# A written order for the prelude and two batches of a Nyström attention and mixture kernel, without filler products

## The chip, the core and the metric

The kernel runs on one core of a Trainium2 chip. The metric is the device time of one execution in microseconds (us). Lower is better. Times of several runs are given as their median.

## What is computed

Three blocks follow one another; their sizes are those of the inputs.

```python
# attention: q, k, v are (8 batches, 8 heads, 576 positions, 64)
q_lm, k_lm = mean of q, k over groups of 18 positions          # 32 landmarks
A, Bm, C = softmax(q k_lm'/8), softmax(q_lm k_lm'/8), softmax(q_lm k'/8)
Z = Bm' / (norm1(Bm) * norminf(Bm) + 1e-6)
for _ in range(6): Z = 2*Z - Z @ Bm @ Z                        # Newton steps
x = A @ Z @ C @ v                                              # as (4608, 512)
# gated block: d_ff = 1536
x = (silu(x @ w_gate) * (x @ w_val)) @ w_out
# soft mixture: 8 experts, 4 slots each
logits = x @ phi;  d = softmax over the tokens, c = softmax over the slots
slot_input = d.T @ x;  slot_out = relu(slot_input[e] @ w1[e]) @ w2[e]
out = c @ slot_out
```

## The kernel before

The work goes through eight batches. A prelude computes the attention of batch 0 (`first_attention`, L424): landmark sums on DVE (`landmark`, L393), score products on TensorE (`scores`, L602; tiles `m_a`, `m_c`), exponentials on ACT, the norm product `m_nx` (L521), five Newton squares (`m_n`, L533) with their side products (`m_T`, L554 and L555), the products with v (`m_v`, L481), and at the end `w_blocks` (L596), which leaves the small matrix `WB`. Beside it runs `a_softmax` (L770): maximum, subtraction on POOL (L792), exponential, sums, multiplication on POOL (L795), a transpose on DVE into `AT` (L789), a copy `EH` rounded by ACT (L797) and the rest `EL` by POOL (L798).

A batch then has twelve units (`unit`, L1020). A unit multiplies the weight product `G` (`g_product`, L812; `GH` by ACT in L837, `GL` by DVE in L851) with `EH` and `EL`: six products into `pg` and six into `pv` for each half (`mm3`, L1011), a gate on ACT (L375) and a product on DVE into `hT` (L1046, or L1044). `logits` (L857) multiplies `hT` for tile `l`. A transpose of `hT` (L871) puts the batch's block into the buffer `HB`. Inside the units of batch b run pieces of the attention of batch b+1 (`attention`, L609) and of the slot sums of batch b-1 (`softmoe`, L902). In batch 0 the weights are converted from double precision as well (`f32_bits`, L237: lines L248, L251 and L252 on DVE, L235 and L242 on ACT), and `w_out` is folded with phi (`m_wt`, `m_p`, `m_ps`; L328, L337, L343).

The slot sums (L985) are 72 products of 32 rows by 32 columns of the array. A product has a place a (which 32 rows) and g (which 32 columns), 16 places in all, and a step k. It takes its part of the exponentials: the tile `DN` itself where a equals g, otherwise a copy in `DR` (the end of buffer `HB_85`) that one of twelve small transfers on the SP queue brought (L951). The transfers are numbered by i = a xor g from 1 to 3 and by a.

SP issues nearly all loads in the order of its instructions; one that has to wait holds those behind it. The other engines are in order too. For the first part of the program a table, `ORDER` (L55), lists for each engine the order of its instructions by their number in the traced program; `written_order` (L123) makes a chain of them. In the kernel before it covers 906 TensorE instructions, 257 on DVE, 180 on ACT, 18 on POOL and 71 on SP, that is the prelude and batch 0. From there to the end the instructions of batch 1 and of the later batches follow the order that the scheduler finds with a few fences.

Filler products: `keep_warm` (L875) multiplies 128 by 128 with 160 columns into a tile nobody reads. `first_attention` calls it four times with four products (L505). At the start 16 products of one element are issued (L1091).

Of the kernel before, what the change touches and what calls it, by code (L numbers as in the profile page):

```python
# [53 lines left out]

ORDER = {  # L55
    'PE': '''
# [7 lines left out]
      788+4 820+6 832+8 814+6 826+6 844+12 862+6 872+16 856+6 888+8 840+4 896+6 920+8''',  # L64
    'DVE': '''
# [8 lines left out]
      239 242+2 238 241 240 247+2 255 252 256+2 253 259 249 246 258 262 261''',  # L74
    'Activation': '''
# [5 lines left out]
      162 167 166 168+2 171 173 170 174 172 175 181 177 176 180 179''',  # L81
    'Pool': '''
      0 2+6 1 8 10 9 11 16 12 15 13+2 17''',
    'SP': '''
      0+2 5 2+2 7 4 6 14 26 8 15 18 10 25 22 17 16 20 9 23 11+3 40 24 19 21 29+2 28 32+2 31 34 36 35 37+3
      42 41 58 43 45 44 27 46 59+2 47+2 61 50+2 49 64 52 65 53 56+2 66+2 54 68+3 55 62 71''',
}


# [1 line left out]
def nystrom_softmoe_kernel(  # L91
# [332 lines left out]
    def first_attention(side):  # L424
# [18 lines left out]
        def c_scores(half):  # L443
            ms = [psp.tile([128, 512], F32, tag="x", name="m_c", bufs=3) for r in range(2)]
            scores(ms, qs, "k", b, half, range(4))
            return ms
# [55 lines left out]
        for r in range(2):  # L502
            c_copy(r, 0, cm[r])
        cm = c_scores(1)
        for _ in range(4):  # L505
            keep_warm(4)
        side("a")
        for r in range(2):
# [366 lines left out]
    def keep_warm(n):  # L875

        m = psp.tile([128, 512], F32, tag="l", name="warm")
        for _ in range(n):
            pe.matmul(m[:, 0:160], ident, cst[:, 128:288], start=True, stop=True)  # L879
# [208 lines left out]
                next(gens[c], None)  # L1088

    m = psp.tile([128, 512], F32, tag="l", name="warm")  # L1090
    for _ in range(16):  # L1091
        pe.matmul(m[0:1, 0:1], one, one, start=True, stop=True)
    first_attention(side)
    in_order("silu", warm, one, AF.Silu)
    for f in side_pre:
# [328 lines left out]
```

## Time and profile before

| | us |
|---|---|
| median of 3 runs (lowest, highest) | 652.75 (651.09, 653.97) |
| profiled execution, its own time | 652.49 |
| its span from first to last instruction | 650.5 |
| prelude, until the first `pg` product | 38.64 |
| batch 0 | 76.27 |
| batch 1 | 69.04 |
| batches 2 and 3 | 65.16, 65.15 |
| busy share of TensorE, DVE, ACT, POOL | 95%, 72%, 46%, 11% |

The stages are cut at the first `pg` product of each batch. The profile gives the busy time of each engine, the clock granted to TensorE, waits by who ended them, and the instructions in order of time. A busy share is an average over stages with different limits, so each stage is read by itself.

### The profile page before, as it was taken

The page shows a single profiled execution, that of the slowest core. Times are in us where ns is not written, and L with a number is a line of the kernel's source. Part 1 is how long each engine was busy: PE and PEld are TensorE (multiplying, and loading weights), DVE is VectorE, ACT ScalarE, POOL GpSimd, SP SyncE. Part 2 cuts the span into 40 slices and gives each one's busy share as a digit, 9 for nine tenths or more (in the row PEclk, how much of TensorE's full clock was granted, in tenths as well). Part 3 has the DMA queues.
Part 4 walks back from the last instruction along what each step waited for, and adds up shares of the span by engine and source line. Part 5 has one row for each costly group of instructions (what it writes and reads, how often), then busy time and mean ns, then how long its engine had stood idle before and what let it go on. Part 6 is the DMA issues. An engine that isn't in the chain of part 4 may idle for free. (4 is left out here: it accounts for less than half of the span.)

```text
span 650.5 us, 18267 instructions
## 1 busy us (share of the span) xinstructions
PE 616.0 (95%) x7591; PEld 465.9 (72%) x7591; DVE 465.8 (72%) x1139; ACT 300.8 (46%) x761; POOL 73.2 (11%) x81
## 2 busy tenths in 40 slices
PE   6889999999999999999999999999999999999990
PEld 3766787777878787878787878787878877743660
DVE  5999898797679687868786878687866555540441
ACT  2787885374256225622562256225723532410540
POOL 0310003021013001300130013001300000010100
PEclk9999999999999999999999999999999999999996
DMA  9997861443042024202420242022310696599999
GB/s 335 390 350 260 341 219 56 164 137 96 7 143 90 2 76 145 90 2 76 145 90 3 74 145 87 6 74 75 100 49 2 218 365 236 191 329 347 348 369 318
DMA packets 63298, 106.47 MB, mean 164 GB/s; under 512 B 4976, under 2 KB 33008, under 8 KB 61680
## 3 DMA queue, kind: packets, MB, share of 16 engines
q1 hardware_dynamic: 63216, 105.32, 48.0%
q8 instruction: 59, 0.97, 0.6%
q14 instruction: 23, 0.19, 0.1%
HBM read 91.24 MB, written 12.58 MB: 160 GB/s over the span
## 5 line engine op out<-in xcount | busy, mean ns | idle before, releaser
L375 ACT ACTIVATE u<-pg 128x288 f32<-128x288 f32 x169 | 69.8, 413 | 152.2 <-PE pg L1017 147.4
L1046 DVE TENSOR_TENSOR hT<-u,pv 128x288 f32<-128x288 f32 x169 | 75.7, 448 | 41.1 <-PE pv L1017 34.9
L1017 PE MATMUL pg<-EH,GH 128*128 128x288 f32 x384 | 92.9, 323 | 0.0
L851 DVE TENSOR_TENSOR GL<-g,GH 128x512 fp32r<-128x512 f32 (+1 forms) x114 | 65.0, 597 | 35.3 <-ACT GH L837 35.3
L1017 PE MATMUL pg<-EH,GL 128*128 128x288 f32 x384 | 84.5, 297 | 0.5
L1017 PE MATMUL pv<-EH,GH 128*128 128x288 f32 x384 | 84.0, 300 | 0.0
L1017 PE MATMUL pg<-EL,GH 128*128 128x288 f32 x384 | 82.1, 295 | 0.0
L1017 PE MATMUL pv<-EL,GH 128*128 128x288 f32 x384 | 82.0, 295 | 0.0
L1017 PE MATMUL pv<-EH,GL 128*128 128x288 f32 x384 | 81.9, 294 | 0.0
L837 ACT CAST GH<-g 128x512 fp32r<-128x512 f32 (+1 forms) x114 | 53.8, 520 | 55.6 <-PE g L820 55.6
L1017 PEld LDWEIGHTS pg<-EH,GH 128*128 128x128 f32 x384 | 59.4, 189 | 23.6 <-issue 20.4
L871 DVE STREAM_TRANSPOSE HB<-hT 128x576 f32<-128x576 f32 x96 | 74.2, 774 | 1.6
L1017 PEld LDWEIGHTS pg<-EH,GL 128*128 128x128 f32 x384 | 62.0, 188 | 2.6 <-DVE GL L851 2.6
L1017 PEld LDWEIGHTS pv<-EH,GH 128*128 128x128 f32 x384 | 61.2, 188 | 3.7 <-issue 2.5
L1017 PEld LDWEIGHTS pv<-EH,GL 128*128 128x128 f32 x384 | 61.5, 188 | 0.0
L1017 PEld LDWEIGHTS pg<-EL,GH 128*128 128x128 f32 x384 | 61.5, 188 | 0.0
L1017 PEld LDWEIGHTS pv<-EL,GH 128*128 128x128 f32 x384 | 61.5, 188 | 0.0
L820 PE MATMUL g<-w,WB 64*32 64x512 f32 (+1 forms) x912 | 55.5, 534 | 1.9 <-DVE GL L851 1.0
L866 PE MATMUL l<-hT,P_sb 128*32 128x160 f32 (+1 forms) x768 | 44.6, 297 | 2.6 <-DVE hT L1046 1.6
L866 PEld LDWEIGHTS l<-hT,P_sb 128*32 128x32 f32 x768 | 15.4, 108 | 40.7 <-DVE hT L1046 14.6
L985 PE MATMUL m_d<-HB,HB 32*32 32x384 f32 x864 | 35.3, 491 | 0.0
L985 PE MATMUL m_d<-HB,DN 32*32 32x384 f32 x288 | 35.1, 491 | 0.0
(254 smaller groups left out, 943.4 us busy)
## 6 DMA issues: line engine op xcount, KB each, us to landing
k<-in_kT_dram SPq DMA_DIRECT2D x52, 288.0 KB, 3.8
ffn<-in_w_dram SPq DMA_DIRECT2D x13, 1024.0 KB, 8.8
ffn<-in_w_dram SPq DMA_DIRECT2D x24, 512.0 KB, 9.0
HB<-in_w_cat_dram SPq DMA_DIRECT2D x8, 1024.0 KB, 8.2
v<-in_v_dram SPq DMA_DIRECT2D x8, 1024.0 KB, 5.9
q<-in_qT_dram SPq DMA_DIRECT2D x28, 288.0 KB, 2.9
HB<-in_w_out_dram SPq DMA_DIRECT2D x12, 512.0 KB, 5.1
wr<-in_w_cat_dram SPq DMA_DIRECT2D x4, 1024.0 KB, 7.6
```

The source lines that it names most:

```text
L375: i = act.activation(*a, **kw)
L820: pe.matmul(gs[r][32 * hp:32 * hp + 32, 0:256 * n].rearrange("p (u f) -> p u f", u=n), WB[b % 2][64 * r:64 * r + 64, hp, :], w[64 * r:64 * ...
L837: act.copy(H_, g)
L851: dve.tensor_tensor(out=GL, in0=g, in1=GH, op=ALU.subtract)
L866: pe.matmul(L[32 * c:32 * c + 32, 0:32 * k], P_sb[:, j, :], main[:, 0:k, c, :], start=j == 0, stop=j == NJ - 1)
L871: dve.transpose(HB[b % 2][:, S * j:S * j + S].rearrange("p (t r) -> p t r", r=32), hT[:, 0:S].rearrange("p (t r) -> p t r", r=32))
L985: pe.matmul(ms[a][32 * g:32 * g + 32, 0:384].rearrange("p (j f) -> p j f", j=NJ), d_of(a, g, k), hb[32 * a:32 * a + 32, :, 4 * k + g, :], ...
L1017: pe.matmul(ps[:, 0:HALF], G_t[b, j, q, sel_][h], e[:, q, ts_], start=n == 0, stop=n == 5)
L1046: i = dve.tensor_tensor(out=o, in0=u, in1=pv[:, 0:HALF], op=ALU.mult)
```

## The change

The table `ORDER` is replaced. It now covers 1306 TensorE instructions, 352 on DVE, 236 on ACT, 22 on POOL and 94 on SP: the prelude, batch 0 and nearly all of batch 1. The 72 slot sums of batch 0, which run inside batch 1, are among them, each by its own number. The 16 filler products of the prelude are gone; the row of one-element products at the start has 31 instead of 16. No instruction that computes something is added or removed, and everything behind the table stands as before.

```diff
 ORDER = {
     'PE': '''
-      0+48 56+4 48+8 60+15 77+4 75+2 81+3 93 84+4 94 88+4 119 95+4 120 92 121+4 99+20 145+2 125+20 147+4
...
+      967+2 993+8 975+12 955+4 987+6 1005+40 1052+6 1064+6 1045+7 1001+4 1058+6 1070+7 1079 1077+2 1081
+      1080 1083 1087 1084 1091 1095 1085 1099 1082 1088 1103 1092 1086 1090 1107 1096 1094 1111 1089 1115
...
         cm = c_scores(1)
-        for _ in range(4):
+        for _ in range(0):
             keep_warm(4)
...
     m = psp.tile([128, 512], F32, tag="l", name="warm")
-    for _ in range(16):
+    for _ in range(31):
         pe.matmul(m[0:1, 0:1], one, one, start=True, stop=True)
```

All lines of the changed kernel stand 14 lines lower. Three places of the order follow.

TensorE in the prelude, from the second half of the `m_c` scores to the first Newton square; before:

```order
L606 MATMUL m_c<-qk_102,qs 32x288 x2
L879 MATMUL warm<-cst 128x160 x12
L521 MATMUL m_nx<-nrm,cst 128x128
L533 MATMUL m_n<-bd 128x128 x2
L471 MATMUL m_t<-cst,CE_161 128x128 x4
L533 MATMUL m_n<-newton 128x128 x2
```

and now:

```order
L620 MATMUL m_c<-qk_102,qs 32x288 x2
L547 MATMUL m_n<-bd 128x128
L535 MATMUL m_nx<-nrm,cst 128x128
L547 MATMUL m_n<-bd 128x128
L485 MATMUL m_t<-cst,CE_176 128x128 x4
L547 MATMUL m_n<-newton 128x128 x5
```

The fillers between the scores and `m_nx` are gone, and so are four that stood between the two halves of the scores.

SP's queue in batch 1, around the twelve transfers from `DN` for the slot sums of batch 0 (`k3`, `q3`, `v3` are loads for batch 3); before:

```order
L219 DMA q3_0_2432<-in_qT_dram 128x576
L219 DMA q3_1_2434<-in_qT_dram 128x576
L219 DMA q3_2_2436<-in_qT_dram 128x576
L951 DMA HB1_85<-DN_81 32x160 x12
L224 DMA v3_2169<-in_v_dram 128x4x512
L225 DMA v3_2169<-in_v_dram 64x512
```

and now, after three of the twelve and the loads of `k3_2` and `k3_3`:

```order
L965 DMA HB1_85<-DN_81 32x160 x4
L233 DMA q3_0_2427<-in_qT_dram 128x576
L239 DMA v3_2164<-in_v_dram 64x512
L320 DMA wo_dram_88<-HB1_85 128x512
L965 DMA HB1_85<-DN_81 32x160 x3
L233 DMA q3_1_2429<-in_qT_dram 128x576
L965 DMA HB1_85<-DN_81 32x160 x2
```

Five of the twelve transfers now stand behind the load of `v3`, whose buffer comes free when the product of batch 2's attention with v (`m_v`, L724) is done.

TensorE in batch 1, the first slot sums (the four tiles `m_d` stand for a = 0 to 3, and `DN` as second operand means a = g); before:

```order
L985 MATMUL m_d_2230<-HB0_84,DN_81 32x384
L985 MATMUL m_d_2231<-HB0_84,HB1_85 32x384
L985 MATMUL m_d_2232<-HB0_84,HB1_85 32x384
L985 MATMUL m_d_2233<-HB0_84,HB1_85 32x384
L985 MATMUL m_d_2230<-HB0_84,HB1_85 32x384
```

and now:

```order
L999 MATMUL m_d_2225<-HB0_84,DN_81 32x384
L999 MATMUL m_d_2228<-HB0_84,HB1_85 32x384
L999 MATMUL m_d_2226<-HB0_84,HB1_85 32x384
L999 MATMUL m_d_2227<-HB0_84,HB1_85 32x384
L999 MATMUL m_d_2226<-HB0_84,DN_81 32x384
L999 MATMUL m_d_2225<-HB0_84,HB1_85 32x384
L999 MATMUL m_d_2228<-HB0_84,HB1_85 32x384 x2
```

Before, the products went through all 16 places in turn. Now the sequence is irregular; the seventh and eighth share a = 3, with g = 1 and g = 2, and the eighth reads the transfer i = 1, a = 3, which is the last of the twelve in SP's new order.

## Rows read from the trace of the kernel before

**Rows 1.** The page: span, busy time of TensorE, granted clock in 40 slices.

```profile
span 650.5 us, 18267 instructions
...
PE 616.0 (95%) x7591; PEld 465.9 (72%) x7591; DVE 465.8 (72%) x1139; ACT 300.8 (46%) x761; POOL 73.2 (11%) x81
...
PEclk9999999999999999999999999999999999999996
```

**Rows 2.** Stages: stretch, length, busy PE, PEld, DVE, ACT, POOL; clock, DMA share, GB/s.

```profile
0.00:38.64 38.64, 28.67 (x344) 20.36 (x344) 30.30 (x72) 20.65 (x46) 9.68 (x13) 1.00 0.98 369
38.64:114.91 76.27, 74.29 (x851) 58.08 (x845) 70.19 (x162) 56.76 (x131) 8.99 (x8) 1.00 0.66 234
114.91:183.95 69.04, 67.22 (x866) 51.80 (x866) 54.36 (x134) 31.19 (x83) 10.61 (x10) 1.00 0.33 105
183.95:249.11 65.16, 64.99 (x826) 51.09 (x825) 51.19 (x127) 29.35 (x77) 8.29 (x8) 1.00 0.25 78
```

**Rows 3.** TensorE's waits in batch 0: total us, times, longest us.

```profile
PE m_ps L343 <- ACT HB L338: 1.3, 1, 1.3
PE g L820 <- DVE GL L851: 1.0, 1, 1.0
```

**Rows 4.** TensorE's waits in batch 1.

```profile
PE l L866 <- DVE hT L1046: 1.0, 1, 1.0
PE l L866 <- DVE hT L1044: 0.6, 1, 0.6
```

**Rows 5.** Busy time in the part of batch 0 with the conversions.

```profile
40.00:100.00 60.00, 58.02 (x695) 44.88 (x692) 56.82 (x134) 48.83 (x111) 3.82 (x3) 1.00 0.76 272
```

**Rows 6.** Timeline of TensorE, prelude: start, length, line, out<-in, count, idle before.

```profile
5.14 1.17 PE L606 MATMUL m_a<-q,ks 64*32 64x288 f32 x4 [3.33 <-DVE ks L396]
...
15.29 4.18 PE L879 MATMUL warm<-cst 128*128 128x160 f32 x24
19.53 0.49 PE L521 MATMUL m_nx<-nrm,cst 128*128 128x128 f32 x2
...
39.01 0.43 PE L1017 MATMUL pg<-EL,GH 128*128 128x288 f32 x2
```

**Rows 7.** Timeline of DVE, ACT and POOL, prelude.

```profile
16.08 0.39 DVE L517 TENSOR_SCALAR nrm<-cst,stat 128x32 f32<-128x32 f32 x2
...
17.90 0.74 DVE L457 TENSOR_REDUCE stat<-CE 128x1 f32<-128x576 f32 x1
...
21.02 0.61 DVE L544 SCALAR_TENSOR_TENSOR newton<-m_n,rc,cst 128x128 f32<-128x128 f32 x2
...
28.76 1.44 DVE L789 STREAM_TRANSPOSE AT<-AN 128x576 f32<-128x576 f32 x2 [0.79 <-POOL AN L795]
...
33.82 0.46 DVE L591 TENSOR_SCALAR VD<-m_v,rc 128x64 f32<-128x64 f32 x2
...
35.42 1.69 POOL L798 TENSOR_TENSOR EL<-AT,EH 128x576 fp32r<-128x576 f32 x1
```

**Rows 8.** Clock: tile m_c (min/median/max ns), stretches of the Newton steps and the end.

```profile
L606 PE MATMUL m_c<-k,qs x16: 402/555/686, 10.8 to 14.9; 64*32 64x288 f32 x16
...
20.50:34.00 13.50, 11.95 (x154) 10.08 (x154) 12.41 (x33) 10.63 (x25) 4.01 (x4) 1.00 1.03 410
...
638.00:640.00 2.00, 0.00 (x0) 0.00 (x0) 0.00 (x0) 0.00 (x0) 0.00 (x0) 0.50 1.09 386
```

**Rows 9.** The transfers from DN in batch 1: issue ns, landing, then SP's timeline.

```profile
L951 SPq DMA_DIRECT2D HB<-DN x12: 582/588/1817, 138.1 to 146.3; - x12
...
DMA to landing us min/median/max: 1.8/2.1/3.7
...
146.98 0.53 SPq L224 DMA_DIRECT2D v<-in_v_dram  x1
```

**Rows 10.** TensorE in batch 1: product with v, then the stretch of the slot sums.

```profile
144.57 1.73 PE L724 MATMUL m_v<-v,CT 128*32 128x64 f32 x80
...
151.90:156.20 4.30, 4.30 (x144) 2.49 (x144) 1.00 0.37 98
```

More of the change, by code (lines that the diff above doesn't have):

```diff
@@ L56 @@
     'PE': '''
[7 rows of a table removed]
-      788+4 820+6 832+8 814+6 826+6 844+12 862+6 872+16 856+6 888+8 840+4 896+6 920+8''',
-    'DVE': '''
[8 rows of a table removed]
-      239 242+2 238 241 240 247+2 255 252 256+2 253 259 249 246 258 262 261''',
-    'Activation': '''
[5 rows of a table removed]
-      162 167 166 168+2 171 173 170 174 172 175 181 177 176 180 179''',
[14 rows of a table added]
+      1288+16''',
+    'DVE': '''
[12 rows of a table added]
+      342 341 350 352+2 318''',
+    'Activation': '''
[7 rows of a table added]
+      231 227+3 232 230 211 233 235 234 236''',
     'Pool': '''
-      0 2+6 1 8 10 9 11 16 12 15 13+2 17''',
+      1 0 2+5 8 7 10 9 11 13 12 15+2 14 18 17 20 19 23''',
     'SP': '''
-      0+2 5 2+2 7 4 6 14 26 8 15 18 10 25 22 17 16 20 9 23 11+3 40 24 19 21 29+2 28 32+2 31 34 36 35 37+3
-      42 41 58 43 45 44 27 46 59+2 47+2 61 50+2 49 64 52 65 53 56+2 66+2 54 68+3 55 62 71''',
+      0+4 5+3 4 25 18 8 17 23 15 9 16 26 22 19 10 14 11+2 21 32 40 20 29 13 30 24 33 31 36 34+2 37 58 28
+      39 42 41 38 59 43+2 27 45 48 47 46 60 51 50 53 52 61 49 55 64 56 65 54 57 62 66+8 81 87 82 74+2 77
+      84 76 83 90 89 63 85+2 78 91 80 79 88 92+2''',
 }
```

50 rows, old and new, of the table ORDER are left out of this document.

## Prediction

> **What bounds the kernel now.** I read the page first: TensorE is busy 616.0 of 650.5 us and its granted clock is full in all slices but the last [rows 1]. An average says nothing about a stage, so I cut the run at the first `pg` product of each batch [rows 2]. The reader is to see four numbers there: the prelude takes 38.64 us with TensorE busy for 28.67, batch 0 takes 76.27, batch 1 69.04, and batch 2 65.16, as do the batches that follow it. From batch 2 on TensorE has 0.2 us of idle time in a batch; there it is the bound, and nothing of it is changed. So what the change gains or loses must be decided before 183.95 us, and arrives at the end unchanged: the order behind it is the same, and the next piece of work is released by the progress of TensorE.
>
> How much is to be had before that point? Batch 1 is 3.88 us longer than batch 2, and the waits of TensorE that the trace names in it are two of `l` for `hT`, 1.0 and 0.6 us [rows 4]. Batch 0 has conversions to do as well: between 40 and 100 us DVE is busy 56.82 of 60 us [rows 5], so DVE and TensorE are both nearly full, and only the 3.18 us in which DVE stands idle can be taken out by order alone. TensorE's two large waits there, 1.3 for `m_ps` and 1.0 for `g`, are of that size [rows 3]. In the prelude TensorE is idle for 10 us, but the chain of small steps is what lasts: norms, Newton steps, `VD`, `WB`, `G`, and beside it the softmax that ends in `EL`.
>
> **The change part by part.** The profiled execution took 652.49 us by its own time; the median of the three runs is 652.75, so the sum below stands 0.26 under what it would be from the median. That is less than the runs differ by.
>
> *Fillers.* The last input of the norm product is written on DVE by 16.47 (two instructions from 16.08, 0.39 together), but TensorE works through 24 filler records from 15.29 to 19.47 and only then starts `m_nx` at 19.53 [rows 6, 7]. DVE had other work to do in those 3 us, reductions of `AN` and `CE`, so the loss is smaller: in the new order three reductions of 576 elements (0.74 each), the two `newton` instructions (0.61) and small ones of some 1.3 in all stand between the last norm input and the end of the second `newton` tile, 4.1 us, and that tile was written at 21.63 before. The Newton steps would begin at about 20.6, 1.0 us earlier. They don't carry this over to the first unit in full. On DVE the two transposes into `AT` (1.44 us), which ran at 28.76, now stand behind `VD`. `VD` ended at 34.28; 1.0 earlier is 33.3. A conversion of some 0.6, the first transpose (0.7), its copy by ACT (0.6) and two `EL` of up to 1.69 on POOL follow, which makes 38.6 for the second `EL`, or 38.3 if the first takes only 1.4. The product that reads it stood at 39.01 [rows 6, 7]. I take **-0.6 us** for the prelude; the bounds are -1.0 (nothing waits for `EL`) and 0.
>
> *One-element products.* 15 more. TensorE stands idle for 3.33 us before the first scores, behind these products, until DVE has a landmark sum [rows 6]. **0**, hidden by the loads and that sum; without this cover they would cost less than 1.
>
> *Clock.* Without the fillers TensorE has almost no work between the end of the scores near 15 and the first Newton square near 20. The same product `m_c` took 686 ns at the beginning and 402 later [rows 8]; I read the long one as the lower level (1.2 GHz), although the profile's clock says 1.00 there. At the end of the run, with TensorE idle after 636, the granted clock is 0.50, which is 1.2 GHz [rows 8]. So an idle stretch can cost the clock, and the Newton steps would start at half rate. From 20.5 to 34 TensorE is busy for 11.95 of 13.50 us [rows 8], but in the new order ACT and DVE set the first steps, with conversions and exponentials between the copies, so a few us at half rate cost little. I take **+0.5**, between 0 and the case below. The Trainium skill, on its page TensorE: Matmul & The Clock Gate (Part 1), says that the low clock is the default, that activity lifts it and that idleness brings it back; it advises against idle gaps between bursts, and so speaks against this change. By the page alone the whole Newton part could begin at the low clock, which is the second rival's time instead of +0.5.
>
> *Batch 0, new order on five engines.* The same instructions, so the same busy time. Bounds: -3.2 (DVE never idle) and 0, or a loss if a wait is planned wrongly (the last rival covers losses). I take half, **-1.6**, because the order of before was written out too and still left 2.3 us of waits on TensorE.
>
> *Batch 1, now written.* Bounds: -3.9 (it becomes like batch 2) and 0. I take the two named waits, **-1.6**.
>
> *Slot sums of batch 0.* Two prices. First the transfers: the eighth product needs the last of the twelve transfers. Five of them stand behind the load of `v3` on SP, which waits for the end of `m_v`. In the trace `m_v` ended at 146.30 [rows 10]. From there SP issues the load of `v3` and two more (0.53 each, by the row of the load of v), and three, then one, of the small transfers (588 ns each) before it issues the last: 1.6 + 2.35 = 3.9 us, and 2.1 until it lands, 6.0 in all [rows 9]. TensorE reaches the first slot sum sooner. Before, it had 24 products of a unit, one `l` and one Newton step between 146.30 and 151.90, 5.6 us with a wait of 1.0 [rows 4, 10]; now the same 24 products and one `l` more (0.3), which is 4.9. Everything behind the eighth product waits, as the engine is in order: 6.0 - 4.9 = **+1.1**, bounds 0.8 and 2.7 by the fastest and slowest landing (1.8 and 3.7). Second the places: 72 products in turn over 16 places took 4.30 us, that is 4.5 rounds of 0.96 [rows 10]. The new sequence breaks into eight runs in which no place repeats (10, 12, 12, 9, 8, 6, 12 and 3 products). If each run cost a round, the last a third of one, it would be 7.0 us, +2.7; if a repeated place cost nothing, 0. I take **+0.7**, nearer the lower end, because a repeated place is held up only by the one product that is still in it.
>
> Sum: -0.6 + 0.5 - 1.6 - 1.6 + 1.1 + 0.7 = -1.5, and 652.49 - 1.5 = **651.0 us**.
>
> **The rivals.**
>
> *The plan holds everywhere.* Prelude -1.0, batch 0 -3.2, batch 1 -3.9, slot sums and clock at 0: 652.49 - 8.1 = 644.4 us. For it: batches 2 to 6 show that this instruction mix runs at 65.2 with TensorE never waiting. Against it: DVE at 95% in batch 0, and the queue of SP as counted above. Chance 0.30, with times from 644 to 649.
>
> *The clock stays low in the Newton steps.* Place: TensorE from 20.5 us on. Price: 11.95 us of products at half rate are 23.9, 10.4 more than the 13.5 that the stretch has, so 652.49 - 2.0 + 10.4 = 660.9 us, the -2.0 being the other terms. If the clock returns in the middle, 655.7. It decides from the point where half-rate products fill the stretch, that is if the clock is low for longer than 3 us beyond 20.5. Against it: scores and fillers in the trace ran at the long duration at first and were at the short one after some 5 us of work, and Newton products are nearly as dense. Chance 0.11; slower.
>
> *Slot sums block TensorE.* The last transfer lands late (+2.7) and each run costs a round (+2.7), and batch 1 gains nothing elsewhere: 652.49 - 1.7 + 5.4 = 656.2 us. For it: the counts above. Against it: in the trace the first products of the next round start before all of the last have ended. Chance 0.10, a third of it within the bound of no change.
>
> **How the numbers follow.** About 0.5%, 3.3 us either side of 652.75 (649.5 to 656.0), is what a measurement can tell from no change. My forecast, 651.0, has 0.49; its own range is 648.5 to 654, and 0.06 of its chance lies under 649.5. Faster: 0.30 + 0.06 = 0.36. Same: 0.43 + 0.03 = 0.46. Slower: 0.11 + 0.07 = 0.18. The range reaches from the floor of the first rival (644) past the third (656.2) and over the half-way case of the clock, to 657; outside lie most of the full clock case and the unlikely gains beyond every bound, less than 2 in 10.
>
> **What would show it.** Right: `m_nx` near 17 and the second `newton` tile near 20.6; the first `pg` near 38; batch 0 near 74.7, batch 1 near 69.2, batch 2 still 65.2; a gap on TensorE after the seventh slot sum that a transfer ends, and a stretch of slot sums over 5 us. Wrong on the clock: `m_n` and `m_T` records of the Newton steps twice as long for more than 3 us, or a row of clock 0.50 between 15 and 38. Wrong on the slot sums: all of them within 4.3 us of the first. Wrong altogether: batch 2 no longer at 65.2, since then something behind the table has moved.

## The result and the profile after

The changed kernel takes 661.2 us (median of 4 runs, 659.07 to 663.47), the kernel before in the same comparison 653.18 us (651.09 to 653.97). The ratio is 1.0134, its 95% interval 1.0117 to 1.0151: slower by 1.3%, where 651.0 with a range to 657 was predicted and slower had a chance of 0.18. The profiled execution took 661.36 us, 8.9 more than that of before.

The page of the changed kernel: span, busy time, granted clock.

```profile
span 659.5 us, 18273 instructions
...
PE 620.0 (94%) x7589; PEld 467.9 (71%) x7589; DVE 466.4 (71%) x1139; ACT 300.8 (46%) x761; POOL 73.0 (11%) x81
...
PEclk9788999998999999999999999999999999999996
```

The clock line, all nines before [rows 1], now has a 7 and three 8s besides the last slice: something before 66 us and near 160 us lowers the clock. The stages, cut at the first `pg` product of each batch, answer to [rows 2]:

```profile
0.00:39.49 39.49, 28.92 (x351) 19.25 (x351) 30.96 (x75) 21.07 (x47) 9.59 (x13) 0.89 0.97 351
39.49:119.92 80.43, 75.37 (x848) 59.23 (x845) 69.64 (x160) 56.38 (x130) 8.88 (x8) 0.97 0.67 236
119.92:193.61 73.69, 69.93 (x860) 53.77 (x858) 54.66 (x133) 30.89 (x83) 10.54 (x10) 0.98 0.29 89
193.61:258.74 65.13, 64.96 (x827) 51.06 (x825) 51.31 (x127) 29.38 (x77) 8.30 (x8) 1.00 0.25 78
```

The prelude is 0.85 us longer, batch 0 4.16, batch 1 4.65; batch 2 is as it was. These make 9.7 us; the stretch from the start of batch 2 to the end gives 0.7 back (465.9 against 466.6 us). Its instructions are the same in all runs, yet it lay between 465.5 and 469.0 us in their profiled executions. In three stages the clock column stands below 1.00. The stretches in question, in the same view:

```profile
16.70:23.50 6.80, 6.09 (x22) 4.88 (x23) 6.61 (x18) 5.94 (x10) 2.94 (x3) 0.50 1.01 407
37.20:40.60 3.40, 3.40 (x28) 1.70 (x27) 2.73 (x6) 3.01 (x7) 1.92 (x2) 0.51 1.01 385
57.60:61.10 3.50, 3.50 (x28) 2.35 (x27) 2.89 (x7) 2.72 (x5) 1.47 (x1) 0.52 0.93 226
160.00:163.50 3.50, 3.50 (x75) 2.35 (x65) 0.18 (x1) 0.00 (x0) 0.04 (x1) 0.52 0.87 331
```

Four times the clock falls to its lower level, 1.2 GHz, while TensorE has work: in the Newton steps, around the first unit, in batch 0 and in the slot sums. The four executions of the changed kernel go by it: 659.07, 661.05, 661.36 and 663.47 us at a mean granted clock of 0.983, 0.979, 0.978 and 0.975.

Ahead of the first fall TensorE had less work than before. The stretch from 13.0 to 16.7 us, before and now:

```profile
13.00:16.70 3.70, 3.65 (x33) 2.54 (x32) 3.02 (x15) 2.13 (x8) 0.00 (x0) 1.00 1.04 415
```

```profile
13.00:16.70 3.70, 1.45 (x20) 0.47 (x16) 3.02 (x14) 3.31 (x10) 0.07 (x1) 1.00 1.05 335
```

**Prelude.** TensorE's timeline, in the order start, length, line, tile; then DVE's:

```profile
16.75 0.79 PE L535 MATMUL m_nx<-nrm,cst 128*128 128x128 f32 x2 [0.52 <-DVE nrm L531]
...
19.90 3.16 PE L547 MATMUL m_n<-newton 128*128 128x128 f32 x10
...
34.47 0.44 PE L613 MATMUL m_w<-newton,VD 128*64 128x128 f32 x4 [0.52 <-ACT newton L571]
...
37.06 1.92 PE L834 MATMUL g<-w,WB 64*32 64x256 f32 x16 [0.97 <-DVE GL L865]
```

```profile
20.11 0.34 DVE L558 SCALAR_TENSOR_TENSOR newton<-m_n,rc,cst 128x128 f32<-128x128 f32 x1
```

TensorE at the same `m_w` before:

```profile
34.40 0.44 PE L599 MATMUL m_w<-newton,VD 128*64 128x128 f32 x4 [0.52 <-ACT newton L557]
```

`m_nx` stands at 16.75, 2.8 us earlier than in [rows 6], and the second `newton` tile is written at 20.45 against 21.63 in [rows 7]. That lead of 1.2 us is gone at `m_w`, which began at 34.40 before and at 34.47 now. The second fall of the clock then stretches the last products ahead of the first unit: 16 `g` records take 1.92 us, 1.47 in the same order at the full clock (the run with the fillers back, below).

**Batch 0.** TensorE's waits, and those of ACT for transfers:

```profile
PE m_ps L357 <- ACT HB L352: 3.5, 2, 2.1
PE m_n L757 <- ACT RV L764: 1.3, 1, 1.3
```

```profile
ACT HB L249 <- DMA wo_dram<-HB: 3.0, 1, 3.0
...
ACT w L249 <- DMA HB<-in_w_cat_dram: 2.5, 2, 1.8
ACT HB L249 <- DMA HB<-in_w_out_dram: 2.0, 1, 2.0
```

By these rows TensorE waits 4.8 us for ACT, and ACT has waited 7.5 us for transfers (7.9 with a fourth row of 0.4); before, ACT's waits for transfers in batch 0 came to 1.8 us. The timeline of ACT shows how the one makes the other:

```profile
56.50 0.66 ACT L249 ACTIVATE HB<-HB 128x512 f32<-128x512 f32 x1 [2.98 <-DMA wo_dram<-HB]
57.07 0.25 ACT L352 COPY HB<-m_p 128x128 f32<-128x128 f32 x1
```

The copy of `m_p`, which TensorE needs for `m_ps`, stands behind a weight conversion that can start only when a store has freed its buffer. TensorE resumes with `m_ps` at 57.37.

**Batch 1.** SP's timeline at the twelve transfers from `DN`, before (see also [rows 9]) and now, then TensorE's:

```profile
138.10 8.79 SPq L951 DMA_DIRECT2D HB<-DN  x12
```

```profile
144.53 2.98 SPq L965 DMA_DIRECT2D HB<-DN  x3
147.61 1.00 SPq L233 DMA_DIRECT2D k<-in_kT_dram  x2
148.66 2.42 SPq L965 DMA_DIRECT2D HB<-DN  x4
151.13 0.58 SPq L233 DMA_DIRECT2D q<-in_qT_dram  x1
151.81 1.48 SPq L239 DMA_DIRECT2D v<-in_v_dram  x1
153.33 0.58 SPq L320 DMA_DIRECT2D wo_dram<-HB  x1
153.96 1.79 SPq L965 DMA_DIRECT2D HB<-DN  x3
155.80 0.58 SPq L233 DMA_DIRECT2D q<-in_qT_dram  x1
156.42 1.14 SPq L965 DMA_DIRECT2D HB<-DN  x2
```

```profile
147.78 1.73 PE L738 MATMUL m_v<-v,CT 128*32 128x64 f32 x80
...
154.62 0.51 PE L999 MATMUL m_d<-HB,DN 32*32 32x384 f32 x1
...
159.25 0.51 PE L999 MATMUL m_d<-HB,HB 32*32 32x384 f32 x2 [3.76 <-DMA HB<-DN]
```

TensorE reaches the slot sums at 154.62, 5.1 us after the end of `m_v`, and stops for 3.76 us until the last transfers land. The 72 products take 11.3 us from first to last instead of 4.30 [rows 10].

### The profile page after: what moved, and what is told of

Read it like the earlier page. It is cut to its first block, busy times and chain, and to the rows that moved or that the text cites. A ratio compares the mean times of both kernels' runs of the same rounds, so it can differ in the third digit from the quotient of the medians.

```text
span 659.5 us, 18273 instructions
## 1 busy us (share of the span) xinstructions
PE 620.0 (94%) x7589; PEld 467.9 (71%) x7589; DVE 466.4 (71%) x1139; ACT 300.8 (46%) x761; POOL 73.0 (11%) x81
## 5 line engine op out<-in xcount | busy, mean ns | idle before, releaser
L1060 DVE TENSOR_TENSOR hT<-u,pv 128x288 f32<-128x288 f32 x169 | 75.6, 448 | 39.3 <-PE pv L1031 33.4
L885 DVE STREAM_TRANSPOSE HB<-hT 128x576 f32<-128x576 f32 x96 | 74.2, 773 | 2.0 <-DMA wo_dram<-HB 0.4
L999 PE MATMUL m_d<-HB,HB 32*32 32x384 f32 x864 | 38.5, 507 | 3.8 <-DMA HB<-DN 3.8
L999 PE MATMUL m_d<-HB,DN 32*32 32x384 f32 x288 | 37.7, 508 | 0.0
```

Source lines behind the costliest of these rows:

```text
L885: dve.transpose(HB[b % 2][:, S * j:S * j + S].rearrange("p (t r) -> p t r", r=32), hT[:, 0:S].rearrange("p (t r) -> p t r", r=32))
L999: pe.matmul(ms[a][32 * g:32 * g + 32, 0:384].rearrange("p (j f) -> p j f", j=NJ), d_of(a, g, k), hb[32 * a:32 * a + 32, :, 4 * k + g, :], ...
L1060: i = dve.tensor_tensor(out=o, in0=u, in1=pv[:, 0:HALF], op=ALU.mult)
```

## The experiments

The table gives, for each run, its median and ratio to the kernel before, and from its profiled execution the length of prelude, batch 0 and batch 1, the stretch of the slot sums, and the stretches before 200 us with a clock of 0.50 (all us). A ratio is to the runs of before in its own comparison, whose medians were 652.3 to 653.2. In the edits, numbers of `ORDER` stand for instructions; a short piece of the list is shown with its runs written out.

| run | median | ratio (95%) | prelude | batch 0 | batch 1 | slot sums | clock 0.50 |
|---|---|---|---|---|---|---|---|
| before (first comparison) | 653.18 | 1 | 38.64 | 76.27 | 69.04 | 4.3 | none |
| changed | 661.2 | 1.0134 (1.0117 to 1.0151) | 39.49 | 80.43 | 73.69 | 11.3 | 17-24, 37-41, 58-61, 160-164 |
| transfers together | 654.8 | 1.0044 (1.0029 to 1.0060) | 39.28 | 78.49 | 69.67 | 5.5 | 19-26 |
| places in turn | 658.4 | 1.0087 (1.0059 to 1.0115) | 39.22 | 80.48 | 72.14 | 9.8 | 15-26, 159-162 |
| both | 656.47 | 1.0067 (1.0046 to 1.0088) | 39.12 | 77.98 | 72.00 | 4.3 | 16-23, 159-166 |
| fillers back | 665.8 | 1.0198 (1.0164 to 1.0231) | 41.91 | 78.75 | 73.34 | 11.0 | 160-164 |
| before, no fillers | 653.33 | 1.0012 (0.9998 to 1.0026) | 39.30 | 77.07 | 69.46 | 4.3 | 17-27 |
| batch 1 unwritten | 654.46 | 1.0028 (1.0016 to 1.0041) | 39.09 | 78.10 | 67.89 | 4.3 | 18-25 |
| old, then batch 1 | 657.07 | 1.0061 (1.0038 to 1.0085) | 38.09 | 75.93 | 73.13 | 8.0 | none |
| the same, together | 654.5 | 1.0028 (1.0013 to 1.0043) | 38.69 | 76.91 | 70.48 | 5.2 | none |
| conversions later | 651.47 | 0.9988 (0.9976 to 0.9999) | 39.25 | 76.67 | 67.88 | 4.3 | 16-23 |
| later and together | 653.81 | 1.0020 (1.0004 to 1.0037) | 39.77 | 76.34 | 71.44 | 5.8 | 16-26, 159-163 |
| fillers in gaps | 653.24 | 1.0019 (1.0002 to 1.0036) | 42.53 | 77.51 | 67.88 | 4.3 | 15-22, 25-29 |
| sum's copy too | 651.57 | 0.9996 (0.9986 to 1.0006) | 38.68 | 75.80 | 67.90 | 4.3 | 16-23 |
| fillers, constants first | 652.86 | 1.0009 (0.9998 to 1.0020) | 39.98 | 76.70 | 67.88 | 4.3 | 21-27 |
| constants first | 652.28 | 0.9998 (0.9988 to 1.0009) | 40.60 | 76.90 | 67.90 | 4.3 | 17-27 |

A profiled execution is one of several, so its stages are read beside the median. Those of "before, no fillers" (656.88), "places in turn" (659.58), "conversions later" (652.64) and "fillers in gaps" (657.44) had the highest times of their runs; those of "fillers back" (662.17), "batch 1 unwritten" (653.95) and "old, then batch 1" (654.66) the lowest.

The first four runs edit the changed kernel.

**Transfers together.** The SP list (76 to 87 are the twelve transfers, 74 and 75 loads of `k3`, 90 and 91 of `q3`, 88 and 89 of `v3`, 63 the store of `wo_dram`):

```diff
-      66+8 81 87 82 74+2 77 84 76 83 90 89 63 85+2 78 91 80 79 88 92+2
+      66+10 81 87 82 77 84 76 83 85+2 78 80 79 90 89 63 91 88 92+2
```

> The changed kernel with one edit in SP's order: the loads of k3_2 and k3_3 stand ahead of the twelve transfers from DN, the loads of q3_0, v3, the store to wo_dram and q3_1 behind them; the twelve follow one another in the order they had. Theory (the queue): the 3.8 us in which the eighth slot sum waits for a transfer goes, the last transfer lands near 155 us, and with the idle stretch gone the clock no longer falls in the slot sums, so their stretch shrinks from 11.3 to about 6 us (4.3 and some 1.6 for repeated places) and the time from 661.2 to about 656. Rival (the places): the stretch is long because places repeat; then it stays over 7 us and the time over 657.5.

The wait for a transfer is gone, the slot sums take 5.5 us and the clock stays full in them:

```profile
152.30:157.90 5.60, 5.60 (x147) 3.72 (x145) 2.33 (x5) 0.00 (x0) 0.00 (x0) 1.00 0.85 241
```

Batch 1 falls from 73.69 to 69.67 and the time by 6.4 us (5.9 by the ratios), more than batch 1 alone gives: the two falls of the clock at 37 and 58 us were absent in this execution too. Falls of the clock differ among its executions: the mean granted clock was 0.987 in this one and another, 0.983 in three. The transfers are the largest single loss.

**Places in turn.** The slot sums in the order of before; SP's queue as changed:

```diff
-      1070+7 1079 1077+2 1081 1080 1083 1087 1084 1091 1095 1085 1099 1082 1088
...
+      1070+84 1160+2
```

> The changed kernel with one edit in TensorE's order: the 72 slot sums of batch 0 go through the 16 places in turn, step by step, as before. SP's order stays. Theory (the queue): a product that needs the last transfer stands within the first round here too, so the wait of about 4 us stays, with the low clock behind it; only the repeated places go, the stretch is 8.5 to 10 us instead of 11.3, and the time about 659. Rival (the places): the stretch falls to 8 us or less and the time to 657.5 or less.

Two waits, 1.16 and 1.92 us, for transfers remain, and the clock falls behind them as before:

```profile
154.20:158.60 4.40, 1.89 (x19) 0.40 (x17) 3.22 (x7) 0.31 (x1) 0.80 (x1) 1.00 0.59 173
158.60:162.00 3.40, 2.83 (x66) 1.55 (x68) 1.67 (x2) 0.00 (x0) 1.52 (x2) 0.52 0.92 256
```

So the places aren't the main loss: with them in turn the stretch is still 9.8 us.

**Both edits.**

> The changed kernel with both edits: transfers together on SP and places in turn on TensorE. Theory: the slot sums take 4.3 to 4.6 us as before, batch 1 comes to 66.5 to 67.5 us, less than the 69.0 of the kernel before, and the time is about 654, what is left being the loss in the prelude and batch 0. Rival (the places of the other wait: removing this wait brings another one of like size in batch 1): batch 1 stays over 69 us.

The slot sums are back at 4.3 us, yet batch 1 takes 72.00 where 66.5 to 67.5 was expected, and more than with the transfers alone: the rival held. TensorE's waits in batch 1 and a stretch behind the slot sums:

```profile
PE m_n L753 <- ACT u L385: 1.3, 1, 1.3
PE m_n L753 <- DVE bd L395: 0.6, 1, 0.6
```

```profile
159.00:165.90 6.90, 6.43 (x34) 4.60 (x35) 4.51 (x10) 1.97 (x5) 0.27 (x1) 0.52 0.23 65
```

Shorter slot sums bring TensorE sooner to the Newton steps of the next batch, where it waits 1.9 us for ACT and DVE in little time, and there the clock fell. The saving was given back by the next wait.

**Fillers back**, all sixteen at the places they had, in the new order:

```diff
-        for _ in range(0):
+        for _ in range(4):
             keep_warm(4)
...
-    for _ in range(31):
+    for _ in range(16):
```

> The changed kernel with the 16 filler products back, four between the halves of the scores and twelve behind them, and 16 one-element products at the start; all else in the new order. Theory (the clock): the clock stays full from about 13 us through the prelude; the Newton squares, 7.5 us in all with the fillers gone, take about 5 us, and the falls of the clock near 37 and 57 us may go too; prelude about 38.5 instead of 39.3, batch 0 shorter by 1 to 2 us, time 658 to 660. Rival (the order): the fillers hold the norm product, DVE and ACT set the Newton steps anyway, and the time stays within 1 us of 661.2.

The clock is full through prelude and batch 0, and batch 0 is 1.7 us shorter. But the prelude is 2.4 us longer, so this execution is 0.8 us slower than that of the changed kernel (662.17 against 661.36). The medians are 4.6 apart; as its time is the lowest of four, the rest isn't in this trace. Four fillers between the halves of the scores wait for their operand, the constants:

```profile
15.02 1.32 PE L893 MATMUL warm<-cst 128*128 128x160 f32 x8 [1.43 <-DMA cst<-in_consts_dram]
```

In the new order SP issues a load of `w_cat` ahead of the constants, and they land 8.8 us after their issue (9.0 in the changed kernel) where it was 6.0 before.

The run also shows the new order of the prelude at the full clock, first on DVE, then on TensorE:

```profile
24.17 0.34 DVE L558 SCALAR_TENSOR_TENSOR newton<-m_n,rc,cst 128x128 f32<-128x128 f32 x1
```

```profile
37.56 0.44 PE L613 MATMUL m_w<-newton,VD 128*64 128x128 f32 x4 [0.52 <-ACT newton L571]
...
40.15 1.47 PE L834 MATMUL g<-w,WB 64*32 64x256 f32 x16 [0.97 <-DVE GL L865]
```

From the second `newton` tile (24.51) to `m_w` it takes 13.05 us here, 14.02 in the changed kernel and 12.77 before; from `m_w` to the first `pg` 4.35, 5.02 and 4.24.

The next runs separate the parts. **Before, no fillers** is the kernel before with the loop over `keep_warm` at 0 and the sixteen numbers taken from its TensorE list.

> The table of the kernel before on all engines; only the 16 filler products are left out. Theory (the lost time of the prelude and of batch 0 lies in the new order, the fillers by themselves are worth little): m_nx 2 to 3 us earlier than 19.53, the granted clock falls to 0.50 for some 7 us of the Newton steps as it did in the changed kernel, prelude 38 to 39.3 us, batch 0 76 to 77, time 651.5 to 653.5. Rival (without fillers the clock costs the time, whatever the order): more than one fall of the clock before 62 us, prelude 39.5 or more and batch 0 78 or more, time 655 to 657.

The fillers are worth 0.1%, at the edge of what can be told from nothing: without them the clock is low for ten of the Newton steps' microseconds, but `m_nx` begins 2.7 us earlier. In the profiled execution the second `newton` tile stands only 0.2 us earlier than before and `m_w` 1.7 later; its time is the highest of twelve, with 2.4 us of the excess behind the start of batch 2, so how the median comes out even isn't shown by it.

**Batch 1 unwritten** is the new order cut back, on each engine, to the numbers that the old table held.

> The new order for the prelude and batch 0 without fillers, cut back to the instructions that the old table lists; batch 1 and the slot sums go by the scheduler again. Theory (two separate losses): prelude and batch 0 as in the changed kernel, 39.3 and 78 to 80.5, but batch 1 69 to 70 with the slot sums in 4.3 to 5 us, no wait for a transfer and the clock full through batch 1; time 655 to 657. Rival (batch 1 is long because batch 0 hands its work over late, whatever is written for batch 1): batch 1 over 72, time 659 or more.

Batch 1 takes 67.89, the shortest of any run until here, 1.15 under before. So the scheduler's batch 1 behind the new batch 0 is good, and the written batch 1 is what costs; batch 0 still loses 1.8. Its waits and ACT's timeline:

```profile
PE m_ps L343 <- ACT HB L338: 2.5, 2, 1.7
PE m_n L743 <- ACT RV L750: 1.3, 1, 1.3
```

```profile
55.51 0.66 ACT L235 ACTIVATE HB<-HB 128x512 f32<-128x512 f32 x1 [2.75 <-DMA wo_dram<-HB]
56.08 0.25 ACT L338 COPY HB<-m_p 128x128 f32<-128x128 f32 x1
```

**Old, then batch 1** lists the old order first, fillers included, and behind it those of the new numbers that the old table lacks. **The same, together** moves the twelve transfers as in the first run.

> The old order with its fillers for the prelude and batch 0, then the new order for the rest of batch 1 with its slot sums and its SP queue. Theory (the loss of batch 1 comes from its own order): prelude 38.6, batch 0 76.3, batch 1 72.5 to 74 with slot sums of 9 us or more, a wait for a transfer of 2 to 4 us and a clock of 0.50 for some 3 us behind it; time 656 to 658. Rival (the new batch 1 fits once batch 0 is on time): DN is there earlier, the wait under 1 us, batch 1 69.5 or less, time 651 to 653.

> As the run before it, and on SP the twelve transfers from DN stand one behind the other again, ahead of the load of v3. Theory (transfers are the main loss of batch 1, as the run with the transfers together showed, and the rest of the new batch 1 is as good as the old): prelude 38.6, batch 0 76.3, batch 1 69 to 70, time 652 to 653.5, no better than before. Rival A (the written batch 1 saves its waits when nothing delays it): batch 1 under 68.5, time under 651.5. Rival B (another wait and a fall of the clock take the place, as with both edits together): batch 1 71 or more, time 654.5 or more.

The first has batch 1 at 73.13, as the theory said, though by less of each part: the wait for a transfer is 1.97 us, the slot sums take 8.0 and no fall of the clock followed. So 4.1 us were lost with a full clock, 3.7 of them in the slot sums. That execution has the lowest time of five; the median is 2.4 us above it. With the transfers together 1.4 us over before remain, 0.9 of them in the slot sums: batch 1 at 70.48 and the time at 654.5 lie above what was expected, batch 1 short of rival B's 71 and the time at its bound. The written batch 1 was better than the scheduler's in neither run. The two parts by themselves, 1.0028 for batch 1 unwritten and 1.0061 for old, then batch 1, make 0.9% of the changed kernel's 1.3%; the rest came only with both, and no run divides it further.

**Conversions later** takes batch 1 unwritten and moves three conversions on ACT behind the copies that TensorE waits for (65, 136 and 152 are the conversions; runs written out):

```diff
-      60 61 65 62 64 75
+      60 61 62 64 65 75
...
-      136 128 129 130 132 138
+      128 129 130 132 136 138
...
-      152 148 151 149 155
+      148 151 149 152 155
```

> As the run with batch 1 unwritten; on ACT three conversions of weights, which stood waiting for a load or a store (2.75, 1.91 and 1.42 us there) in front of the copies and scalings that TensorE waits for, now stand behind these: one L235 behind the L338 copy and u, one L235 behind two L750, u and L344, one L235 behind L338, u and L758. Theory (the loss of batch 0 is ACT, in order, held by late transfers): the waits of TensorE for ACT in batch 0, 1.66 + 1.34 + 0.87 = 3.9 us, go; batch 0 from 78.1 to 74.2 to 75.5, batch 1 near 68, time 650 to 652, under the kernel before. Rival (DVE, which works on the conversions next, is the bound and becomes late instead): TensorE waits for hT, GL or g in place of the copies, batch 0 still over 77, time 653.5 to 655.

TensorE's waits of 3.9 us for these copies are gone. The largest that is left in batch 0 is

```profile
PE m_c L606 <- ACT P_sb L344: 0.9, 1, 0.9
```

Batch 0 falls by 1.4 us, to 76.67, and not to the expected 74.2 to 75.5: this and smaller waits take the place of a part, and TensorE is busy for 74.77 us of the batch instead of 73.88; why it is busy longer isn't shown. The profiled execution falls by 1.3 us (653.95, the lowest, to 652.64, the highest of its run) and the median by 3.0 (2.6 by the ratios). That is the first version under the kernel before, by 0.1%, which is less than the 0.5% that the prediction took as its bound.

**Later and together** puts the two repairs into the changed kernel.

> The changed kernel with two edits: the twelve transfers from DN together on SP, and the three conversions on ACT behind the copies that TensorE waits for. Theory (the two losses of the changed kernel stand beside each other and add): against the run with the transfers together alone (654.8, batch 0 78.49, batch 1 69.67) batch 0 loses 3 to 4 us of waits, 74.5 to 75.5, batch 1 69.7, time 651 to 652.5. Rival (what batch 0 saves, batch 1 gives back, since its Newton steps and transfers then collide with other work, as with both earlier edits together): batch 1 71.5 or more, time 653 to 655.

Batch 0 gains 2.2 us (76.34) instead of 3 to 4, and batch 1 gives 1.8 back (71.44: two waits of `m_n`, 0.7 and 0.6 us, and a low clock from 159.3 to 162.7), as in the run with both edits. The time is the rival's, and batch 1 lies just under its 71.5. Of the 8.0 us that the changed kernel lost against before, 1.5 are left (653.81 beside 652.29).

**Fillers in gaps** and **sum's copy too** start from the conversions later:

```diff
-        for _ in range(0):
-            keep_warm(4)
+        for n in (4, 2):
+            keep_warm(n)
```

> As the run with the conversions later, with six filler products that hold nothing up: four in the gap of 1.4 us between the two halves of the scores and two in the gap of 0.65 us behind them. Theory (the fall of the clock is what eats the earlier start of the Newton steps): no stretch of clock 0.50 in the Newton steps, their squares as short as before, m_nx still near 17, prelude 37.9 to 38.4 in place of 39.08, time about 0.8 to 1.0 us less, 650.4 to 650.8. Rival A (six fillers don't keep the clock up): the same fall as there, prelude 39, time 651.3 to 651.8. Rival B (the clock stays full but the prelude is bound by the softmax, DVE and POOL): no fall, prelude still 38.8 or more.

The fillers did hold something up: they waited 2.77 us for the constants, and everything behind them too, so the theory wasn't tested. The other moves the copy of `m_ps` (67) ahead of two conversions:

```diff
-      62 64 65 75 67 68
+      62 64 67 65 75 68
```

> As the run with the conversions later, with two of them one place further back, behind the copy of m_ps (L344), for which m_c waited 0.87 us in batch 0 there. Theory (any wait of TensorE in batch 0 that ACT's order makes can be taken out): batch 0 from 76.67 to 75.8, time 650.3 to 650.8. Rival (DVE, which takes over the conversion, is then late by the same amount): batch 0 76.5 or more with a new wait on DVE, time 651.3 or more.

Batch 0 took 75.80, of which TensorE is busy 75.18, and the profiled execution 650.96 us. Stages of this run:

```profile
0.00:38.68 38.68, 27.87 (x350) 18.81 (x350) 30.32 (x74) 20.48 (x46) 9.27 (x13) 0.91 0.95 350
38.68:114.48 75.80, 75.18 (x848) 58.14 (x845) 70.23 (x161) 56.38 (x132) 9.16 (x9) 1.00 0.72 255
114.48:182.38 67.90, 66.45 (x859) 51.88 (x858) 53.84 (x133) 30.86 (x83) 10.61 (x10) 1.00 0.32 96
```

The median, 651.57 beside 652.42, is within the bound of no change and above the 650.3 to 650.8 that was expected.

**Fillers, constants first** and its control move the load of the constants (8) ahead of those of `w_cat` (25) and `w_out` (18) on SP; the first has the six fillers as well:

```diff
-      0+4 5+3 4 25 18 8 17 23
+      0+4 5+3 4 8 25 18 17 23
```

> As the run with the sum's copy moved too, with the six filler products of the run before it, and the load of the constants, which the fillers read, issued on SP ahead of the loads of w_cat and w_out (there the fillers waited 2.77 us for it). Theory (the fall of the clock ate the earlier start of the Newton steps): the fillers run in the gap between the halves of the scores, no 0.50 in the Newton steps, m_nx near 17, prelude 37.5 to 38.0 in place of 38.52, time 650.4 to 651.0. Rival (another chain bounds the prelude, or the Newton steps start later than without fillers): prelude 38.4 or more though the clock is full, time 651.3 or more.

> The same order of SP without fillers, as the control: the earlier constants alone. Both theories: nothing waits for the constants but the masks of the norms, so prelude 38.3 to 38.7 with the clock at 0.50 for about 7 us of the Newton steps, time 651.3 to 651.8, the same as with the sum's copy alone.

Now the fillers ran at 13.32 without a wait, and the clock was full until about 20.5; then it fell all the same:

```profile
13.00:20.40 7.40, 5.31 (x44) 3.62 (x40) 6.64 (x26) 6.70 (x15) 1.74 (x2) 1.00 1.03 376
20.40:27.20 6.80, 6.02 (x26) 5.68 (x27) 6.18 (x18) 4.48 (x11) 1.70 (x2) 0.51 1.04 380
```

Between 16.5 and 20.7 TensorE stood idle four times for 0.5 to 0.7 us. Six fillers move the fall, they don't prevent it. The control's prelude was 40.60 in its profiled execution, against the expected 38.3 to 38.7, with a low clock from 17.2 to 27.4; 0.8 of the 1.9 us over the run without the edit stand ahead of `m_nx` (17.42 against 16.63), 1.1 between the second `newton` tile and `m_w`, where the clock was low for 10 us instead of 7; what made the fall longer isn't settled. So what a prelude with the early start and a full clock would take wasn't measured.

## Why the prediction was wrong

The sum had six terms; against the profiled executions they came out as follows.

*Fillers, -0.6.* The mechanism was right: `m_nx` near 17, the second `newton` tile at 20.45 (20.6 was predicted), `VD` at 33.2 (33.3). The gain didn't reach the first unit, for the most part because of the clock, not of `EL`: 39.49 instead of 38. With the stretches of the run with the fillers back the first `pg` would stand at 20.45 + 13.05 + 4.35 = 37.85, an estimate.

*One-element products, 0: right.* They took 1.68 us instead of 0.93, and the first scores began at 5.10 against 5.14.

*Clock, +0.5: the term that was mis-sized first.* The working said that ACT and DVE set the first Newton steps, "so a few us at half rate cost little". From the second `newton` tile to `m_w` the changed kernel took 14.02 us, the same order at the full clock 13.05, so the first fall cost 1.0. The later falls weren't in the sum at all. From `m_w` to the first `pg` it took 5.02 us against 4.35 at the full clock, 0.7 for the second fall ahead of batch 0; batch 0 without its named waits took 75.6 us (80.43 - 4.8) with two falls, 74.5 with none (78.49 less waits of 1.37, 1.32 and 1.34 in the run with the transfers together), so another 1.1; the slot sums up to 1.7, which is what 3.4 us at half the clock can lose (11.3 less the wait of 3.8 and the 5.5 of the run with the transfers together leave 2.0). Together that is an estimate of 4.5 us. The second rival had the place right but priced it at one place only, and its full case didn't come: the low clock lasted about 3 us beyond 20.5, the length from which it said that the clock decides, though some 17 us in all four falls together. The statement of the Trainium skill on its page TensorE: Matmul & The Clock Gate (Part 1), that activity lifts the clock and idleness lowers it, agrees with the rows of the prelude: between 13.0 and 16.7 us TensorE was busy 3.65 us before the change and 1.45 after, and behind it stood 1.00 and 0.50. In the old order the fillers' removal, with its earlier start and its lower clock, comes to 0.1% (1.0012). So the removal by itself is not the loss.

*Batch 0, -1.6: wrong sign, +4.2.* The step was "half of DVE's idle time can be taken out by order". It looked at TensorE and DVE alone. That a wait might be planned wrongly was said, and left to the last rival, which has no price for batch 0: the sum's bound there was 0. ACT, idle for a quarter of the batch, became the engine that blocks: in order, with a conversion at its head that waits for a load or a store. The run with the conversions later shows this as the cause of 3.9 us of waits. Two smaller faults stood beside it: the wait of 1.0 us for `GL` in [rows 3] ends at 38.05, in the prelude, so batch 0 had less to give; and the stage row already limited the gain to 76.27 - 74.29 = 2.0 us, since TensorE's busy time doesn't shrink.

*Batch 1 waits, -1.6: not borne out.* Outside the slot sums batch 1 took 73.69 - 11.3 = 62.4 us, before 69.04 - 4.3 = 64.7: -2.3. But this gain stood only beside the long stop in the slot sums (62.3 to 62.4 also with the fillers back and with the places in turn), in which other engines went on: from 155 to 159 us DVE was busy for 3.35 of 4.0 us. Where the slot sums weren't held up, the same part of the new order took 64.1 us (transfers together), 65.6 (later and together) and 67.7 (both edits), with waits of 1.3 to 1.9 us in the Newton steps. The scheduler gained 1.15 behind the new batch 0 without any written order.

*Slot sums, transfers +1.1: 3.8 of wait.* The mechanism was right (a wait after the first products that the last transfer ends, TensorE there 5.1 us after `m_v`, 4.9 predicted), the size was not. The step that failed is "from there SP issues": the count began at the end of `m_v` as if SP stood waiting there. SP came to the load of `v3` only at 151.81, 2.3 us after `m_v` had ended, busy since 144.53 with the seven transfers and three loads ahead of it. From its first transfer to the end of its last issue it took 13.0 us (144.53 to 157.56), before 8.8 for the twelve alone; and the load of `v3` took 1.48 us to issue, not 0.53. SP's issuing was the bound, and `DN` set its start: the first transfer began 6.4 us later than before (144.53 against 138.10), while `m_v` ended only 3.2 later.

*Places, +0.7.* With the transfers in time the stretch was 5.2, 5.5 and 5.8 us in three runs against 4.3, so +0.9 to +1.5: within the bounds and a little over the value. The third rival named this place and gave 656.2; it lacked the fall of the clock that followed the wait here.

One run comes out at the sum's -1.5, with ACT's conversions behind the copies and batch 1 left to the scheduler: 650.96 against 652.49 in the profiled executions. That is luck. Its parts are 0.0 in the prelude, -0.5 in batch 0 and -1.1 in batch 1, which are not the sum's, and in the medians (0.9996) it can't be told from no change. A gain of the plan wasn't shown; what late transfers cost it in two places was.

## What to carry to other kernels

A written order fixes what each in-order queue does when a transfer is late: put instructions that wait for a load or a store behind the small copies that the busiest engine needs, and count the queue of the engine that issues transfers from its first instruction, not from the event that it waits for. Price a wait on TensorE with the fall of the clock that may follow it. Where a scheduler does as well, as in batch 1 here, leave it free to do so.

## What the runs showed that was not expected

The clock fell behind several short gaps, not only behind a long one: 1.13, 0.65 and 0.52 us before the fall at 16.7. It isn't the same in each execution of similar work: after waits of 0.68 and 0.64 us in batch 1 it stayed full in the run with the transfers together and fell in the run later and together. The executions of the latter run also lie further apart, from 650.38 to 655.95 us, than those with the conversions later alone, 650.28 to 652.64.

A small transfer took SP 588 ns to issue at the median in the changed kernel, up to 1713, and the load of `v3` 1.48 us: an issue is work of the queue, and it varied threefold.
